# Float32 products on halves of the array in place of high and low parts

## The chip, the cores and the metric

The kernel runs on one core of one Trainium2 chip. The metric is device time in microseconds, as the median of several executions; a separate execution is recorded by the hardware profiler, and all rows below come from that one. PE is TensorE (matrix products), PEld its weight loads, DVE is VectorE, ACT is ScalarE, POOL is GpSimd, SP is the engine that issues the transfers. SBUF is the on-chip working memory and PSUM the eight banks of 128 partitions x 512 float32 into which TensorE writes.

## The reference

Random-feature attention, and behind it a feed-forward layer with softplus. The inputs are float32 except the two weights of the feed-forward, which the kernel gets as float64 words.

```python
# q, k, v: (8, 8, 576, 64); omega: (128, 64); w_in: (512, 2048); w_out: (2048, 512)
q_s, k_s = q * D ** -0.25, k * D ** -0.25
def phi(x):
    h = x @ omega.T - sum(x * x) / 2
    return exp(h - max(h)) / sqrt(128)
q_p, k_p = phi(q_s), phi(k_s)              # (b, h, 576, 128)
kv = k_p.T @ v;  z = sum(k_p)              # per head: 128 x 64, 128
x  = (q_p @ kv) / (q_p @ z + 1e-6)         # heads side by side: 4608 x 512
g  = softplus(x @ w_in)
out = g @ w_out                            # 4608 x 512
```

## The kernel before

**Feed-forward.** The 4608 tokens are taken in 13 blocks, three of 256 tokens and ten of 384. A block goes in 16 steps, one for each 128 of the 2048 hidden features. In a step the first layer multiplies four chunks of 128 inputs; each float32 operand is held as two float32r parts, a high and a low one, and three of the four products of parts are made (lines 765 to 767: 12 matmuls on the block's tokens). ScalarE and VectorE make the softplus of the result out of PSUM (771, 774, 777, 780), split it into parts (784, 788), and the second layer multiplies them with three matmuls of 512 columns for each 128 tokens (794 to 796), which add up in PSUM over the 16 steps.

**Attention.** Four heads make a quad, two quads a batch, so there are 16 quads. A quad's keys or queries are handled in five units, four of two 128-token tiles and one of one tile (of two heads side by side). A tile holds two heads: the transposed rows of one head on partitions 0 to 63, those of the other on 64 to 127. A unit is loaded, projected with omega, its row maxima and norms are taken, and ScalarE makes the exponentials (440), one instruction for each of the unit's columns of heads. Keys: the exponentials are multiplied with v and a column of ones (514), which adds up over a quad to kv and z. Queries: VectorE sums the products with z (595), inverts (600), POOL divides (604), TensorE transposes (611), and the result is multiplied with kv (673 and 674) to give the feed-forward's input, which is written as a high part `xh` (699) and a low part `xl` (702).

**Two forms of the projection.** For the first two batches (`NB = 2`; four quads) `project` (397) multiplies a tile by a 128 x 256 matrix in float32 that holds omega twice, with zeros between, so that both heads come out of one product. For the other six batches the transposed rows are loaded twice, on both halves of the partitions (331), rounded to a high part (364), and the low part takes the place of one half (368); `project_two` (407) then multiplies both parts at once with each part of omega, ScalarE copies one half of the result (414), and VectorE adds the other to it and takes the maximum on the way (419). The rows for the norms are loaded once more (355) and squared (375 or 377). Likewise only the first batch (`FN = 1`) multiplies queries with kv in float32 (`plan_x`, 723): two matmuls with 64 columns of weights, one for each half of the array's columns. The others split the queries (626, 630) and kv (538, 544), make four matmuls for each pair of heads (673, 674), and fold the halves with a copy (679) and an addition (682).

**Order.** All instructions of an engine stand in one order, written out before the kernel runs. Each piece of work (`Work`) has the engines that can do it with a cost for each, a due time, what it follows, and the buffers that it takes and gives back. `in_order` simulates the engines with these costs: the engine that can start first takes the earliest due of the works that can start, and a buffer is taken by the one that starts. Due times of attention spread it over about the first five sixths of the feed-forward's steps. PSUM's eight banks are named: two `at`, two `h` (first layer), three `acc` (second layer), one `kv`. Attention of the first batch may take any of `at`, `h` and `acc`; the later batches take `at` alone. SP issues the loads in the order of the plan, and a load waits for its buffer.

Of the kernel before, what the change touches and what calls it, by code (L numbers as in the profile page):

```python
# [28 lines left out]
FN = 1  # L29
NB = 2           # the batches before which the tensor engine has time to spare  # L30
RING = 2 * S     # tokens that the feed-forward's input holds
# [7 lines left out]
SLOW = 6.83      # until when the tensor engine's clock is at half its rate  # L39
# [4 lines left out]
CK, CQ = 0, 1  # L44
VW = (256 if CK else 512) + 4 * (D + 1)   # of one unit of the first batch: the heads' transposed keys, then their values
# [23 lines left out]
def in_order(works, room, ahead, margin):  # L69
    """The works in an order that keeps the engines busy: each engine, once free, takes the  # L70
    earliest due of those that can start. room: the buffers of each kind; ahead: how far from
    the earliest one left a work may be due; margin: how late data may come to the tensor engine."""
# [7 lines left out]
    held = {}          # buffer: the times from and to which it is taken  # L80
# [4 lines left out]
    def start(w):  # L85
        """when, where and with which buffers"""
# [41 lines left out]
def with_fill(out, held, banks, until, emit):  # L128
    """The same with something for the tensor engine to do where it waits, lest its clock go down"""
# [14 lines left out]
def favor_softplus_kernel(ctx, tc, q0, k0, qx, kx, qs, ks, qn, kn, vv, om, om2, wi, wo, out):  # L144
# [19 lines left out]
    idle = at.tile([P, P], F32, name="idle", tag="hl.0", bufs=1)  # L164
# [10 lines left out]
    # the features' weights, high and low parts: of one head on both halves of the rows; of two heads,  # L175
    # zeros between, for the first batches, where later the last rows of theirs go
    oms = const.tile([P, 2, M], F32R, name="oms")
# [11 lines left out]
    # each [P, DM] chunk of the weights: its float64 words, then in their place its two parts  # L189
# [27 lines left out]
    two = {}  # L217

    def load_two():
        two["f"] = ff.tile([P, 512], F32, name="omf2", tag=two["t"], bufs=1)[:, :M]  # L220
        nc.sync.dma_start(two["f"], om2)

    def two_parts():
        f = two["f"]
        nc.vector.tensor_scalar(f, f, float(D) ** -0.25, None, ALU.mult)
        nc.vector.tensor_copy(oms[:, 0], f)
        nc.vector.tensor_tensor(oms[:, 1], f, oms[:, 0].bitcast(F32), ALU.subtract)

    two_done = do("SP", 0.55, 81.62, load_two, take=[("t2", two, "t")], delay=DL)
    two_done = do("DVE", 0.5, 81.62, two_parts, after=[two_done], give=[(two, "t")])  # L230

    in_w = []          # the words that come where the parts go have gone

    def plan_weights(nm, fc, due):
        """float64 words to float32, rounded, in place; then to two float32r parts, exactly"""
# [4 lines left out]
        def load():  # L240
            # all chunks' parts fill the buffers: the last words are in another
# [5 lines left out]
        def low_bits(e):  # L247
            # the three bits of the low word that float32 has room for, rounded
# [6 lines left out]
        def rebias(e):  # L255
            # the exponent from a bias of 1023 to one of 127: what is under 2**-119 goes to zero
# [44 lines left out]
    # ---- attention: one quad = four heads = two pairs of heads  # L301
# [9 lines left out]
    prev = {}          # the latest unit's works: units follow each other  # L311

    def plan_unit(q, kind, u, due, early):
        """one unit of a quad's keys or queries: [P tokens, (head parity, pair), M]"""
        nm = f"{kind}{q.nm}_{u}"
        first = q.b < NB
        cols = early and {"k": CK, "q": CQ}[kind]
        if first:
            src = (k0 if kind == "k" else q0)[q.qd] if early else (kx if kind == "k" else qx)[q.b - 1, q.qd]
        else:  # L320
            src, src_nat = ((ks, kn) if kind == "k" else (qs, qn))
            src, src_nat = src[q.b - NB, q.qd], src_nat[q.b - NB, q.qd]
# [4 lines left out]
        def load():  # L327
            if not first:
                x = at.tile([P, UW], F32, name=f"x{nm}", tag=b["x"], bufs=1)[:, : n * P]
                for r in range(2):  # L330
                    nc.sync.dma_start(x[r * D : (r + 1) * D], src[:, u * UW : u * UW + n * P])
                b["raw"] = x
                return
            if early:
                # the exponentials come where the rows were
# [4 lines left out]
                if cols:  # L340
                    b["raw"], b["nat"] = x[:, 2 * P : 2 * P + w], x[:, :w]
                    c = VW if kind == "k" else w
                    nc.sync.dma_start(x[:, 2 * P : 2 * P + c], src[:, u * (VW if kind == "k" else 2 * P) :][:, :c])
                else:
                    c = VW if kind == "k" else UW
                    b["raw"], b["nat"] = x[:, :w], x[:, w : 2 * w].rearrange("p (c d) -> p c d", d=D)
                    nc.sync.dma_start(x[:, :c], src[:, u * c : u * c + c])
# [5 lines left out]
        def load_nat():  # L353
            b["nat"] = at.tile([P, 4, D], F32, name=f"n{nm}", tag=b["nats"], bufs=1)[:, :n]
            nc.sync.dma_start(b["nat"], src_nat[:, 4 * u : 4 * u + n])

# [3 lines left out]

        def high(e):
            t = at.tile([P, 4 * P], F32R, name=f"hl{nm}", tag=b["hls"], bufs=1)
            b["hi"], b["lo"] = t[:, : n * P], t[D:, : n * P]
            (nc.scalar.copy if e == "ACT" else nc.vector.tensor_copy)(b["hi"], b["raw"])
# [649 lines left out]
```

## Time and profile before

| | |
|---|---|
| three executions | 1172.12, 1176.93 (median), 1177.15 us |
| span of the profiled execution | 1173.2 us |
| PE, busy in the span | 1090.2 us (93%) |
| PEld | 969.7 us (83%) |
| DVE | 839.2 us (72%) |
| ACT | 778.8 us (66%) |
| POOL | 597.7 us (51%) |
| moved by DMA | 93.09 MB |

The page gives no time beside the span for the profiled execution; its span lies 3.7 us under the median of the three. Matmuls overlap, since each has a long way through the array: a matmul's duration is not what it costs, and the distance from its start to the start of the next one is. That is why 93% busy does not say how full PE is. In the timeline, a row of several instructions (x4) has the start of the first one and the time up to the end of the last.

### The profile page before, as it was taken

To read this page: it belongs to the slowest core of one execution; us is meant where nothing else is said; L and a number is where in the kernel's file an instruction comes from. 1 tells how busy PE (TensorE), PEld (TensorE's weight loads), DVE (VectorE), ACT (ScalarE), POOL (GpSimd) and SP (SyncE) were. 2 spreads that over 40 slices of the span, in tenths; PEclk is the share of its full clock that TensorE was granted. 3 is DMA by queue.
4 is the path that set the end of the run, shared out by engine and by line. 5 is a ranking of instruction groups with operands and counts; after the bars stand their busy time and mean duration, and the time that the engine had idled before them with its cause. 6 is when DMAs were issued, how large, how long until landed. Compare 5 with 4: busy or idle time off the path is not lost.

```text
span 1173.2 us, 20521 instructions
## 1 busy us (share of the span) xinstructions
PE 1090.2 (93%) x6094; PEld 969.7 (83%) x6094; DVE 839.2 (72%) x2842; ACT 778.8 (66%) x2061; POOL 597.7 (51%) x630
## 2 busy tenths in 40 slices
PE   8776889999998899999999999999998999999998
PEld 8655778888787788888898898888897888899997
DVE  7999997788878877877777777877786788311111
ACT  5566667777776666677777786666675667555544
POOL 4657764555555555555456555455553454322222
PEclk8889889999999999999999999999999999999999
DMA  9642123342323232232332231332222220000000
GB/s 356 226 127 90 42 77 89 80 113 79 86 79 94 68 100 57 71 100 64 78 88 75 64 105 57 82 92 60 73 85 69 58 82 23 1 28 1 28 1 28
DMA packets 66543, 93.09 MB, mean 79 GB/s; under 512 B 10880, under 2 KB 40320, under 8 KB 66432
## 3 DMA queue, kind: packets, MB, share of 16 engines
q1 hardware_dynamic: 66432, 91.78, 26.7%
q8 instruction: 49, 0.80, 0.3%
q14 instruction: 62, 0.51, 0.1%
HBM read 82.28 MB, written 9.47 MB: 78 GB/s over the span
## 4 chain that ended last, share of the span: by engine, by line
PE 44%; DVE 36%; ACT 11%; issue 6%; DMA 2%; POOL 1%; SPq 0%; DVEq 0%; ACTq 0%; POOLq 0%
DVE junk L595 7%; PE h L765 6%; PE h L766 6%; PE h L767 6%; PE acc L794 6%; PE acc L795 6%; PE acc L796 6%; ACT phk L440 3%; PE kv L514 3%; DVE smk L433 2%; DVE u L780 2%; DVE phq L419 2%; DVE phk L419 2%; ACT phq L440 2%; DVE smk L428 2%
## 5 line engine op out<-in xcount | busy, mean ns | idle before, releaser
L788 POOL TENSOR_TENSOR gl<-u,gh 128x384 fp32r<-128x384 f32 (+1 forms) x205 | 202.0, 986 | 280.0 <-ACT gh L784 219.5
L765 PE MATMUL h<-xh,wi 128*128 128x384 f32 (+1 forms) x832 | 278.8, 335 | 17.9 <-DVE u L780 17.7
L766 PE MATMUL h<-xl,wi 128*128 128x384 f32 (+1 forms) x832 | 272.2, 327 | 1.0 <-DVE xl L731 1.0
L767 PE MATMUL h<-xh,wi 128*128 128x384 f32 (+1 forms) x832 | 271.9, 327 | 0.0
L794 PE MATMUL acc<-wo,gh 128*128 128x512 f32 x576 | 230.9, 401 | 0.0
L795 PE MATMUL acc<-wo,gh 128*128 128x512 f32 x576 | 226.1, 392 | 1.2 <-DVE wo L280 1.2
L796 PE MATMUL acc<-wo,gl 128*128 128x512 f32 x576 | 225.7, 392 | 0.0
L780 DVE SCALAR_TENSOR_TENSOR u<-h,u 128x384 f32<-128x384 f32 (+1 forms) x208 | 108.5, 522 | 160.7 <-ACT u L777 157.4
L765 PEld LDWEIGHTS h<-xh,wi 128*128 128x128 f32 x832 | 159.2, 191 | 27.5 <-DVE u L780 22.8
L771 ACT ACTIVATE u<-h 128x384 f32<-128x384 f32 (+1 forms) x208 | 96.9, 466 | 124.3 <-PE h L767 104.4
L595 DVE CUSTOM_DVE_ANT_0 junk<-phq,zb 128x128 f32<-128x128 f32 x280 | 149.2, 533 | 29.8 <-ACT phq L440 4.2
L766 PEld LDWEIGHTS h<-xl,wi 128*128 128x128 f32 x832 | 159.5, 192 | 5.0 <-DVE xl L731 1.2
L767 PEld LDWEIGHTS h<-xh,wi 128*128 128x128 f32 x832 | 159.2, 191 | 0.0
L796 PEld LDWEIGHTS acc<-wo,gl 128*128 128x128 f32 x576 | 108.6, 188 | 24.3 <-POOL gl L788 0.3
L795 PEld LDWEIGHTS acc<-wo,gh 128*128 128x128 f32 x576 | 108.8, 189 | 14.7 <-DVE wo L280 1.7
L794 PEld LDWEIGHTS acc<-wo,gh 128*128 128x128 f32 x576 | 108.8, 189 | 13.9 <-issue 0.5
L440 ACT ACTIVATE phk<-phk,smk 128x128 f32<-128x128 f32 x216 | 69.8, 391 | 75.2 <-DVE smk L433 71.7
L604 POOL TENSOR_TENSOR phq<-phq,dnq 128x512 f32<-128x512 f32 (+1 forms) x69 | 66.3, 962 | 84.2 <-DVE dnq L600 49.7
L774 ACT ACTIVATE u<-u 128x384 f32<-128x384 f32 (+1 forms) x208 | 104.4, 502 | 4.3
L440 ACT ACTIVATE phq<-phq,smq 128x128 f32<-128x128 f32 x216 | 69.8, 392 | 55.6 <-DVE smq L433 55.4
L777 ACT ACTIVATE u<-u 128x384 f32<-128x384 f32 (+1 forms) x208 | 104.4, 502 | 3.5
L784 ACT CAST gh<-u 128x384 fp32r<-128x384 f32 (+1 forms) x181 | 87.8, 485 | 28.0 <-DVE u L780 17.4
(130 smaller groups left out, 2012.3 us busy)
## 6 DMA issues: line engine op xcount, KB each, us to landing
xk<-ks SPq DMA_DIRECT2D x96, 128.0 KB, 2.7
xq<-qs SPq DMA_DIRECT2D x96, 128.0 KB, 2.8
out<-o SPq DMA_DIRECT2D x36, 256.0 KB, 2.1
vk<-vv SPq DMA_DIRECT2D x70, 130.0 KB, 2.4
rawi<-wi SPq DMA_DIRECT2D x16, 512.0 KB, 6.2
rawo<-wo SPq DMA_DIRECT2D x16, 512.0 KB, 4.3
nk<-kn SPq DMA_DIRECT2D x48, 128.0 KB, 2.4
nq<-qn SPq DMA_DIRECT2D x48, 128.0 KB, 2.6
```

Source lines behind the costliest of these rows:

```text
L440: nc.scalar.activation(b["ph"][:, c], x[:, c], AF.Exp, bias=b["sm"][:, 2, c : c + 1])
L595: nc.vector.tensor_tensor_reduce((b["junk"][:, c] if "junk" in b else junk)[r], b["ph"][r, c], q.zb[r, h], 1.0, 1e-6, ALU.mult, ALU.add, d ...
L765: nc.tensor.matmul(b["h"], wh, xh[:, cc, t], start=cc == 0, stop=False)
L766: nc.tensor.matmul(b["h"], wh, xl[:, cc, t], start=False, stop=False)
L767: nc.tensor.matmul(b["h"], wl, xh[:, cc, t], start=False, stop=cc == NCC - 1)
L774: nc.scalar.activation(b["u"], b["u"], AF.Exp, scale=-1.0)
L777: nc.scalar.activation(b["u"], b["u"], AF.Ln, bias=1.0)
L780: nc.vector.scalar_tensor_tensor(b["u"], b["h"], 0.0, b["u"], ALU.max, ALU.add)
L788: (nc.vector if e == "DVE" else nc.gpsimd).tensor_tensor(b["gl"], b["u"], b["gh"].bitcast(F32), ALU.subtract)
L794: nc.tensor.matmul(acc[tt], gh, w2[fc][:, 0], start=fc == 0, stop=False)
L795: nc.tensor.matmul(acc[tt], gh, w2[fc][:, 1], start=False, stop=False)
L796: nc.tensor.matmul(acc[tt], gl, w2[fc][:, 0], start=False, stop=fc == NFC - 1)
```

## The change

The features' products are made in float32 for all eight batches, and so are the products of queries and kv; high and low parts stay in the feed-forward only.

- Projection: for each tile two matmuls in place of one or two. Each takes one head: 64 rows of the array (partitions 0 to 63, or 64 to 127), the head's transposed rows as weights, omega as the moving operand with 128 columns. The two write to two banks, one for each head, so a unit takes two banks at once, and gives them back when its exponentials are done. The maxima are taken by two reductions, one for each bank; the exponentials read PSUM.
- Queries times kv: `plan_x`, unchanged, for all batches. The splits of rows, queries and kv, the copies and additions that joined the parts, and the second and third load of the rows are gone. The low part `xl` is now always made by VectorE, out of PSUM.
- z goes through memory transposed, so that each head's z lies in consecutive words when VectorE reads it.
- Four buffers of rows (`x`) instead of two. The second batch may use the `acc` banks too (`more`).
- Costs in the plan: the diff has them.

```diff
     def act(n, space=None):
-        return (0.054 if space == PSUM else 0.094) + 0.000833 * n
+        return (0.066 if space == PSUM else 0.105) + 0.000833 * n
...
         def project():
+            both = [bank(f"pp{nm}_{j}", b["ppb", j]) for j in range(2)]
+            b["pp"] = [x[:, : nt * M].rearrange("p (t m) -> p t m", m=M) for x in both]
+            b["rest"] = both[0][:, 2 * M :]
             for t in range(nt):
-                o = b["pp"][:, 2 * t : 2 * t + 2, :]
-                nc.tensor.matmul(o, b["raw"][:, t * P : (t + 1) * P], omf, start=True, stop=True)
+                for j in range(2):
+                    r = slice(j * D, (j + 1) * D)
+                    nc.tensor.matmul(
+                        b["pp"][j][:, t], b["raw"][r, t * P : (t + 1) * P], omf[r, j * M : (j + 1) * M],
+                        start=True, stop=True,
+                    )
+            if cols:
+                b["sm"] = at.tile([P, 3, 4], F32, name=f"sm{nm}", tag=b["sms"], bufs=1)
+                b["ss"] = b["rest"][:, :n]
+                for t in range(nt):
+                    nc.tensor.matmul(
+                        b["ss"][:, 2 * t : 2 * t + 2], b["nat"][:, t * P : (t + 1) * P], halves, start=True, stop=True
+                    )
-        def maxima():
-            nc.vector.tensor_reduce(b["sm"][:, 1, :n], b["pp"][:, :n], AX.X, ALU.max)
-        def project_two(t):
...
-        def aside(t):
...
-        def sums(t):
...
+        def maxima(j):
+            nc.vector.tensor_reduce(b["sm"][:, 1, j:n:2], b["pp"][j], AX.X, ALU.max)
...
-            x = b["pp"] if first else b["ph"]
-            for c in range(n):
-                nc.scalar.activation(b["ph"][:, c], x[:, c], AF.Exp, bias=b["sm"][:, 2, c : c + 1])
+            for t in range(nt):
+                for j in range(2):
+                    c = 2 * t + j
+                    nc.scalar.activation(b["ph"][:, c], b["pp"][j][:, t], AF.Exp, bias=b["sm"][:, 2, c : c + 1])
...
+        kind_ = BANKS.get(q.b, "at")        # BANKS = {0: "any", 1: "more"}
+        p = do(
+            "PE", 0.12 + (0.44 if cols else 0.215) * nt, due + 0.53, project, after=[ld] + ([s] if cols else []),
+            behind=prev.get("project"),
+            take=[(kind_, b, ("ppb", 0)), (kind_, b, ("ppb", 1))] + (sm if cols else []) + ([] if early else [("ph", b, "phs")]),
+        )
...
+        m = do("DVE", dve(nt * M), due + 0.01, lambda: maxima(0), after=[p, r])
+        m = do("DVE", dve(nt * M), due + 0.01, lambda: maxima(1), after=[m], give=[] if early else [(b, "x")])
         m = do("DVE", dve(n), due + 0.41, less_norms, after=[m])
-        m = do("DVE", dve(n), due + 0.42, bias, after=[m], give=[(b, "ssb")] if cols else [])
+        m = do("DVE", dve(n), due + 0.42, bias, after=[m])
         e = do(
-            "ACT", n * (act(M, PSUM if first else None) + 0.09), due + 0.42, exponent, after=[m],
-            give=[(b, "sms")] + ([(b, "ppb")] if first else []),
+            "ACT", n * 0.26, due + 0.42, exponent, after=[m],
+            give=[(b, "sms"), (b, ("ppb", 0)), (b, ("ppb", 1))],
         )
...
         def out_z():
-            q.zd = dram.tile([P, 4], F32, name=f"zd{q.nm}", tag="zd", bufs=2)
-            nc.sync.dma_start(q.zd, q.z)
+            q.zd = dram.tile([4, M], F32, name=f"zd{q.nm}", tag="zd", bufs=2)
+            nc.sync.dma_start(q.zd.rearrange("c m -> m c"), q.z)
...
         for p in range(2):
-            cc = 2 * q.qd + p
-            if q.b < FN:
-                plan_x(q, due, cc, o, w, t0, any_, qt, p)
-                continue
...
+            plan_x(q, due, 2 * q.qd + p, o, w, t0, any_, qt, p)
...
-                "PE", 0.0025 * n + 0.013, due, lambda ccs=ccs: layer1(ccs),
+                "PE", 0.00254 * n + 0.063, due, lambda ccs=ccs: layer1(ccs),
-                "PE", 0.653, due + 6.38, lambda tt=tt: layer2(tt),
+                "PE", 0.68, due + 6.38, lambda tt=tt: layer2(tt),
...
-    counts = {"w": 2 * NFC, "t2": NT2, "x": 2, "nat": 2, "v": 2, "hl": 2, "sm": 4, "ph": 4, "z": 2, "zb": 2, "dn": 4}
+    counts = {"w": 2 * NFC, "t2": NT2, "x": 4, "v": 2, "sm": 4, "ph": 4, "z": 2, "zb": 2, "dn": 4}
...
+    room["more"] = room["at"] + room["acc"]
```

More of the change, by code (lines that the diff above doesn't have):

```diff
@@ L214, in do @@
         return w
[L217 to L230, printed above, removed]
     in_w = []
@@ L450, in plan_unit @@
             ldv = do("SP", 0.55, due - 5.26 + .1, load_v, behind=ld, take=[("v", b, "vs")], delay=DL)
-        lds = ld
-        if not first:
-            lds = do("SP", 0.55, due - 3.95, load_nat, behind=ld, take=[("nat", b, "nats")], delay=DL)
-        wx, h, l = n * P, None, None
-        s = do(("POOL", "ACT"), (pool(w), act(w)), due, squares, after=[lds])
-        if not first:
-            h = do(
-                ("DVE", "ACT"), (dve(wx, 2), act(wx)), due, high, after=[ld], behind=prev.get("high"),
-                take=[("hl", b, "hls")],
-            )
-            l = do(
-                ("DVE", "POOL"), (dve(wx), pool(wx)), due + 0.1, low, after=[h], behind=prev.get("low"), give=[(b, "x")],
-            )
-            prev.update({"high": h, "low": l})
@@ new lines, in plan_unit @@
+        s = do(("POOL", "ACT"), (pool(w), act(w)), due, squares, after=[ld])
+        r, sm = None, [("sm", b, "sms")]
+        if not cols:
+            r = do("DVE", dve(w), due + 0.2, norms, after=[s], behind=prev.get("norms"), take=sm)
+            prev["norms"] = r
+        kind_ = BANKS.get(q.b, "at")
[4 more added lines that the diff above has]
+        )
@@ L518, in plan_keys @@
         q.kvm = do(
-            "PE", 0.855, due + 1.6, outer, after=[e, ldv, q.kvm], take=[("acc" if q.n == 1 else "kv", q.slots, "kv")] if u == 0 else [],
+            "PE", 0.9, due + 1.6, outer, after=[e, ldv, q.kvm], take=[("acc" if q.n == 1 else "kv", q.slots, "kv")] if u == 0 else [],
             give=[(b, "x")] if early else [(b, "phs"), (b, "vs")],
@@ L645, in plan_queries @@
         h = do(
-            ("ACT", "DVE"), (act(n * M, PSUM), dve(n * M)), due + 1.1, high, after=[t],
-            give=[(b, "tpb")] if q.b < FN else [],
-        )
-        if q.b >= FN:
-            h = do("DVE", 0.6, due + 1.1 + .1, low, after=[h], give=[(b, "tpb")])
+            ("ACT", "DVE"), (act(n * M, PSUM), dve(n * M)), due + 1.1, turned, after=[t], give=[(b, "tpb")],
+        )
         q.turned.append(h)
```

226 lines of the change are left out of this document (34 added, 192 removed).

## The prediction

> **What bounds the kernel now.** I read the stages first, because the work changes twice. The windows give busy time for each engine in each stretch; the second line names the columns.
>
> ```profile
> core 0 of [0], span 1173.2 us
> core 0: us, PE busy (x) PEld busy (x) DVE busy (x) ACT busy (x) POOL busy (x), PEclk, DMA share, GB/s
> 0.00:200.00 200.00, 161.49 (x911) 138.39 (x912) 186.46 (x434) 123.54 (x342) 124.49 (x122) 0.90 0.43 144
> 200.00:1000.00 800.00, 760.05 (x4328) 677.96 (x4326) 622.02 (x2349) 567.64 (x1541) 428.62 (x464) 1.00 0.28 77
> 1000.00:1173.00 173.00, 168.62 (x858) 153.33 (x858) 30.73 (x62) 87.60 (x178) 44.56 (x45) 1.00 0.04 14
> ```
>
> DVE fills the first 200 us (186 of 200). The last 173 us hold the feed-forward almost alone. The 800 us between hold all attention of batches 2 to 7, and there no engine is full. The same windows for line 765 alone, four of whose matmuls make a step of the feed-forward, show how many steps each stretch did:
>
> ```profile
> 0.00:200.00 200.00, 32.58 (x99) 20.59 (x99) 0.90 0.43 144
> 200.00:1000.00 800.00, 194.21 (x580) 109.67 (x580) 1.00 0.28 77
> ```
>
> PE's timeline gives what a step costs, from start to start: one step of the tail, four products of 256 columns, and a stretch with one projection, four transposes and eight products of keys with v.
>
> ```profile
> 1080.64 0.34 PE L765 MATMUL h<-xh,wi 128*128 128x384 f32 x1
> ...
> 1082.73 0.39 PE L794 MATMUL acc<-wo,gh 128*128 128x512 f32 x1
> ...
> 1084.77 0.34 PE L765 MATMUL h<-xh,wi 128*128 128x384 f32 x1
> ```
>
> ```profile
> 598.11 0.28 PE L673 MATMUL xp<-qhq,kvs 128*128 128x256 f32 x1
> ...
> 598.58 0.34 PE L765 MATMUL h<-xh,wi 128*128 128x384 f32 x1
> ```
>
> ```profile
> 608.84 0.63 PE L407 MATMUL ppq<-oms,hlq 128*128 128x256 f32 x4
> 609.31 0.34 PE L765 MATMUL h<-xh,wi 128*128 128x384 f32 x1
> ...
> 611.05 0.60 PE L611 MATMUL tpq<-ident,phq 128*128 128x128 f32 x4
> 611.48 1.00 PE L514 MATMUL kv<-vk,phk 128*128 128x65 f32 x8
> 612.29 0.48 PE L794 MATMUL acc<-wo,gh 128*128 128x512 f32 x1
> ```
>
> A step of 384 tokens takes 4.13 us. One of 256 has 12 matmuls of 0.117 (0.47 / 4) and six of 0.227 (2.04 / 9): 2.77. The 580 matmuls are 145 steps. There are 48 small steps, 99 / 4 = 25 of them done before, so 23 x 2.77 + 122 x 4.13 = 568 us of the 800. Attention on PE, by the code's counts for a quad: 18 tiles of projection at 0.235, five times 0.9 for kv (0.81, and 0.09 by which the next matmul's row is longer than its like), 18 transposes at 0.11, eight products of 0.117 and eight of 320 columns, 0.147 in proportion: 4.2 + 4.5 + 2.0 + 2.1 = 12.8, for 12 quads 154. So PE computes 722 us and waits 78 in this stage. How the waits go with DVE is seen in two stretches; first all engines, then line 765:
>
> ```profile
> 400.00:500.00 100.00, 93.31 (x513) 82.39 (x514) 77.65 (x281) 66.64 (x178) 54.22 (x59) 1.00 0.30 78
> 600.00:700.00 100.00, 97.94 (x561) 89.43 (x560) 72.34 (x293) 76.55 (x205) 56.20 (x61) 1.00 0.32 90
> ```
>
> ```profile
> 400.00:500.00 100.00, 23.00 (x68) 12.95 (x69) 1.00 0.30 78
> 600.00:700.00 100.00, 24.88 (x73) 13.70 (x73) 1.00 0.32 90
> ```
>
> 17 steps are 70 us, with a share of 154 / 8 = 19 for attention 89: 11 us of waits at DVE 78%. 18.25 steps leave 5.5 at DVE 72%. The bound of the stage is PE's own work plus waits for a chain that runs through DVE, ACT and POOL.
>
> **What leaves those engines.** The groups of the whole kernel (busy, mean ns | idle before):
>
> ```profile
> L419 DVE CUSTOM_DVE_ANT_0 phk<-ppk,phk 128x128 f32<-128x128 f32 x216 | 52.0, 283 | 3.9 <-ACT phk L414 3.4
> L682 DVE TENSOR_TENSOR x<-xp,x 64x256 f32<-64x256 f32 (+1 forms) x112 | 50.9, 454 | 37.6 <-ACT x L679 35.7
> L630 DVE TENSOR_TENSOR qlq<-tpq,qhq 128x512 fp32r<-128x512 f32 (+1 forms) x84 | 45.1, 551 | 30.7 <-ACT qhq L626 30.5
> L364 DVE CAST hlk<-xk 128x512 fp32r<-128x512 f32 (+1 forms) x40 | 24.1, 603 | 5.6 <-PE ppk L407 5.2
> L368 POOL TENSOR_TENSOR hlk<-xk,hlk 64x512 fp32r<-64x512 f32 (+1 forms) x57 | 67.5, 1183 | 24.4 <-ACT hlk L364 5.4 <-issue 4.1 <-DVE hlk L364 3.9
> L702 POOL TENSOR_TENSOR xl<-x,xh 128x256 fp32r<-128x256 f32 (+1 forms) x56 | 46.0, 825 | 41.9 <-ACT xh L699 36.3 <-PE ppq L407 5.2 <-PE xp L674 0.2
> L731 DVE TENSOR_TENSOR xl<-xp,xh 128x256 fp32r<-128x256 f32 (+1 forms) x8 | 3.5, 445 | 0.0
> ```
>
> L419, L364 and L368 have a twin for queries of about the same size. DVE loses 2 x 52 + 51 + 45 + 2 x 24 = 248. It gains `xl`, 56 x 0.445 = 25, and 240 reductions, two for a unit. One of 256 columns out of PSUM is the smallest of line 400, 0.39 us; 240 x 0.39 = 94 at most, since a fifth are half as wide:
>
> ```profile
> L400 DVE TENSOR_REDUCE smk<-ppk x20: 387/678/683, 6.6 to 192.6; 128x4 f32<-128x512 f32 x16, 128x2 f32<-128x256 f32 x4
> ```
>
> Net -129, nearly all in the stage: 622 becomes 493, 62% of 800. ACT loses the copies of lines 414 and 679, POOL 2 x 67.5 + 46 = 181 of its 598 (the three stretches' sum). DVE gains once more from that: its tiny bias instruction takes 0.13 us where it starts at once and 0.45 in the median, and I ascribe the difference to POOL's use of the memory that both read; the bound from below is no gain.
>
> ```profile
> L428 DVE SCALAR_TENSOR_TENSOR smk<-smk x80: 132/450/1260, 7.6 to 955.8; 128x4 f32<-128x4 f32 x64, 128x2 f32<-128x2 f32 x16
> ```
>
> So DVE ends near 55 to 60%. Two stretches give 5.5 us of waits less for 5 points of DVE, which can't go on to below zero; what remains even in the good stretch are hand-overs. I take 3 in 100 us, half of the good stretch, thus 24 in the stage; the bounds are 0 and the 78 of now.
>
> The third load of the rows and the second copy leave SP's queue (one transfer for a unit in place of three, 240 fewer), and a load there is queued no longer behind POOL's splits. That I cost at nothing: DMA is 28% busy. The transposed z costs SP a transfer in pieces of four bytes, 14 times, under the units of the next quad's keys; should it land late, line 595 of one unit waits on DVE, 14 times, and PE with it only if the next transposes are due by then.
>
> **What PE gains and loses.** The trace has no matmul on half of the rows. It has the kin on half of the columns, line 723; PE, then PEld:
>
> ```profile
> 92.00 1.30 PE L723 MATMUL xp<-qq,kvs 128*64 128x320 f32 x8 [1.56 <-DVE xl L731]
> 93.23 0.50 PE L794 MATMUL acc<-wo,gh 128*128 128x512 f32 x1
> 93.57 0.39 PE L795 MATMUL acc<-wo,gh 128*128 128x512 f32 x1
> ```
>
> ```profile
> 93.23 0.19 PEld L794 LDWEIGHTS acc<-wo,gh 128*128 128x128 f32 x1 [0.49 <-issue]
> ```
>
> Four float32 products stand there as eight matmuls, two passes each. In fp32r a pass of 320 columns is 0.147 us, and eight one after the other at twice that (a float32 column at half the rate) would be 2.35. They took 1.23 to the next start: four pairs of 0.27, so the halves run at the same time. And there is a price: 1.23 - 4 x 0.267 leaves 0.16, of which some 0.05 is the first, half-wide weights' load and 0.1 an empty array; then the next matmul needs 0.34 to its successor in place of 0.227, because its weights were not loaded ahead. Leaving the halves costs 0.1 + 0.11 = 0.21 us. Entering full-width weights on half of the rows I take as the same 0.21, all entries here having stood in a wait; the bounds are 0 and 0.21.
>
> A two-tile unit then has four slots. A slot streams 128 float32 columns (0.267 x 128 / 320 = 0.107) under a load that takes as long (kv's slot, 0.9 / 8 = 0.11): 0.44 + 0.42 = 0.86 against 0.47 now. 96 such units x 0.39 and 24 of one tile x (0.22 + 0.42 - 0.235) = 0.4 are +47 us in the stage. Products with kv, two pairs of heads in one visit: 4 x 0.213 or 4 x 0.267 and 0.37 of entering and leaving, against 8 x 0.117 or 8 x 0.147: +0.28 or +0.26, 24 visits, +6 (and +9 more if every pair makes a visit of its own).
>
> The Trainium skill, TensorEngine Tiling (Array Packing), Key Properties, says that changing the tiling mode drains the TensorE, while other tiles of the same mode run independently; the exit at 93.23 agrees with its 0.1 us. By the page alone (drains without the reload) the stage would pay 120 x 0.2 = 24, an estimate, in place of 47, and end where half of the price does below.
>
> **The sum.** Stage: 568 + 154 + 47 + 6 + 24 = 799 against 800. First 200 us, bound by DVE: batch 1 loses L630, L682 and half a dozen small ones for five query units, 5 x (0.55 + 0.7), and gains 15 x 0.1 of reductions and 4 x 0.445 of `xl`: -3; z read in consecutive words saves 0.11 (369 to 255, the smallest of each kind) on 20 to 40 of line 595, -3. Its PE work in wide float32 projections (0.86 for a unit too) does not change. Tail: nothing, no part of it is touched.
>
> ```profile
> L595 DVE CUSTOM_DVE_ANT_0 junk<-phq,zb x280: 369/392/1509, 159.0 to 999.8; 128x128 f32<-128x128 f32 x112, 64x128 f32<-64x128 f32 x28
> L595 DVE CUSTOM_DVE_ANT_0 xq<-xq,zb x40: 255/281/1414, 30.6 to 78.4; 128x128 f32<-128x128 f32 x32, 64x128 f32<-64x128 f32 x8
> ```
>
> That is -7, and 1166 for the span of 1173.2. Not every change of mode is paid in full: where PE stands in a wait before a projection, the empty array lies in it, and I take off 3. Span 1163, and with the 3.7 us by which the median lies over this span, 1167.
>
> **Rivals.** (a) The switches cost little: row halves take weights ahead while full-width matmuls run. Then 47 + 6 falls to about 0, the stage is 568 + 154 + 24 = 746, the time 1173 - 54 - 9 + 4 = 1114; with half of the price 1140. For it: the trace shows the price on columns only. Against: the exit has the same neighbours. (b) Slower: banks. A unit takes both `at` banks from its projection to its last exponential: 0.86 + two reductions 0.8 + two tiny instructions 0.9 + four exponentials, about 1.2, and four hand-overs of 0.15 make 4.4 us, where a unit is due every 800 / 120 = 6.7, and transposes (0.6 and a copy) and kv products need the same two banks. It decides from about 2 us of queueing on DVE and ACT: then each projection, which stands in PE's fixed order, waits. At 0.3 us for each of 120: waits 24 + 36 = 60, span 1199, time 1203. For it: two banks replace one, held more than twice as long. Against: DVE and ACT get emptier. (c) Row halves don't run at the same time: 8 slots in place of four, +0.44 x 96 + 0.22 x 24 = +47, time 1214. Against: line 723. (d) The waits fall only to those of the good stretch, 5.5 in 100, 44 in all: 1167 + 20 = 1187, and with the half-price switches of (a) to 1160.
>
> **Chances.** Forecast 0.35, (a) 0.17, (b) 0.2, (c) 0.08, (d) 0.2. What a measurement of this kernel tells from no change is about 0.5%, 6 us. Of the forecast's 0.35 (1157 to 1177) 0.24 are faster, 0.11 within it; (a) is faster; (d) spreads over all three, 0.06, 0.07, 0.07; (b) and (c) slower. Together faster 0.47, same 0.18, slower 0.35. The range goes from half-way into (a) to (b): 1128 to 1203; the likeliest case's own is 1152 to 1180.
>
> **What would show it.** Right: projections start in pairs a few ns apart, a unit takes 0.44 us plus gaps, and the weights after it are loaded late, 0.2 us; DVE in the stage at 55 to 62%, POOL under 45%; PE's waits at 24 us, mainly before projections and transposes. Wrong: no gap after a projection (a); long waits of a projection on ACT's exponentials (b); starts 0.11 apart (c); DVE still over 70%, or the first 200 us changed by more than 15 us, which nothing here foresees.

## The result, and the profile after

The changed kernel takes 1275.97 us (median; 1274.27 to 1277.25) beside 1175.47 for the kernel before: a ratio of 1.0852, with a 95% interval of 1.0822 to 1.0881. It is slower by 100 us. The forecast was 1167, and 1275.97 lies outside its range. Of the kernels below, the first with an extra write was traced in an execution that took 1418 us at a granted clock of 0.735; its time leaves that execution out, its landing times come from it. The loss lies in the stage with attention. The windows of the kernel after (busy time per engine, then the granted clock, the DMA share and GB/s):

```profile
core 0: us, PE busy (x) PEld busy (x) DVE busy (x) ACT busy (x) POOL busy (x), PEclk, DMA share, GB/s
200.00:1000.00 800.00, 737.18 (x4348) 617.47 (x4347) 375.96 (x1339) 394.37 (x1040) 239.67 (x299) 0.95 0.27 54
200.00:1100.00 900.00, 828.14 (x4851) 693.13 (x4850) 423.74 (x1502) 444.06 (x1166) 269.20 (x334) 0.95 0.27 53
```

DVE, ACT and POOL did lose their work. But PE is idle for 72 of the 900 us, and its mean clock is 0.95 where it was 1.00. The same windows for line 595 of this kernel, one of the three products of the first layer, count the steps: 532 / 4 = 133 in 800 us, where the kernel before made 145.

```profile
200.00:1000.00 800.00, 183.84 (x532) 102.38 (x531) 0.95 0.27 54
```

The chain that ended last, from the page, has a share of transfers, and by line the first of them is the load of the queries' rows:

```profile
PE 73%; DMA 11%; DVE 9%; issue 4%; ACT 1%; POOL 1%; SPq 0%; POOLq 0%; DVEq 0%; ACTq 0%
PE acc L624 10%; PE h L595 10%; PE h L596 9%; PE h L597 9%; PE acc L625 9%; PE acc L626 9%; DMA xq<-qx 8%; PE kv L424 5%; PE ppq L348 4%; PE ppk L348 3%; PE xp L553 3%; PE tpq L506 2%; DVE xq L490 2%; DMA xk<-kx 1%; DMA zd<-z 1%
```

Among the DMA issues, z's write to memory stands out. The last number is the median time from issue to landing. The first fence is of before, the second of after, with the loads of the queries' rows for comparison:

```profile
zd<-z SPq DMA_DIRECT2D x14, 2.0 KB, 1.9
```

```profile
xq<-qx SPq DMA_DIRECT2D x56, 256.0 KB, 2.8
...
zd<-z SPq DMA_DIRECT2D x14, 2.0 KB, 10.3
```

The same 2 KB, 14 times, take 10.3 us instead of 1.9. The trace after tells the landing of one of the 14 only, but z's read, which waits for the write, is issued 9.9 to 12.6 us behind it all 14 times, and 1.4 to 4.4 us in the kernel before. What follows from one of them is seen around 626 us. SP's timeline after (start, duration, issue), then the chain in that stretch (start, us), then the timelines of PE, DVE and ACT:

```profile
626.46 0.38 SPq L460 DMA_DIRECT2D zd<-z  x1
626.93 0.46 SPq L325 DMA_DIRECT2D vk<-vv  x1
627.51 0.36 SPq L320 DMA_DIRECT2D xq<-qx  x1
638.03 0.33 SPq L464 DMA_DIRECT2D zb<-zd  x1
638.46 0.37 SPq L320 DMA_DIRECT2D xk<-kx  x1
```

```profile
627.51 12.81 DMA xq<-qx
...
640.39 0.62 POOL xq L332
641.01 2.13 issue
643.14 0.66 PE tpq L506 x2
```

```profile
635.77 0.34 PE L597 MATMUL h<-xh,wi 128*128 128x384 f32 x1
643.14 0.66 PE L506 MATMUL tpq<-ident,phq 128*128 128x128 f32 x2 [7.04 <-issue]
```

```profile
641.04 0.42 DVE L337 TENSOR_REDUCE smq<-xq 128x4 f32<-128x256 f32 x1 [8.52 <-POOL xq L332]
```

```profile
642.16 1.14 ACT L382 ACTIVATE phk<-ppk,smk 128x128 f32<-128x128 f32 x4 [9.37 <-DVE smk L374]
```

Two things happen at once. SP stands at `zb<-zd` (it needs z's write), with the load of the next keys behind it, until 638. And the queries' rows, issued at 627.51, before SP stood, are on their way for 12.81 us, where 2.8 is the median. POOL squares them late, and DVE, whose order is fixed, stands for 8.52 us at the sum of these squares (line 337). The unit of these rows is projected only at 651.83. But behind line 337, in DVE's order, stand the small norm instructions of the keys' unit before it, so ACT waits 9.37 us before the exponentials of that unit (line 382), and until they are done the unit holds both `at` banks. PE's next piece of work, two transposes, needs such a bank: its data were ready at 632, and it starts at 643.14, as the exponentials let go of the first bank. PE, whose order is fixed as well, stops for 7 us. That it waits for the bank is argued from the plan and these times; PE's row names no engine for the wait. DVE waits like this, for 7 to 8.5 us, behind each of the 13 writes of z after 200 us, once for a unit of keys and else for queries, whose waits add up to (us in all, times, longest):

```profile
DVE smq L337 <- POOL xq L332: 95.5, 13, 8.5
```

Behind the stop of PE the clock is lower for a while, as the windows around the same place show:

```profile
636.00:643.00 7.00, 0.10 (x1) 0.00 (x0) 1.30 (x5) 0.84 (x4) 1.11 (x2) 0.73 0.47 90
643.00:645.00 2.00, 1.86 (x10) 1.89 (x10) 0.42 (x1) 1.74 (x7) 1.07 (x2) 0.50 0.00 0
645.00:647.00 2.00, 2.00 (x7) 1.25 (x9) 0.56 (x1) 0.33 (x1) 0.00 (x0) 0.50 0.29 64
...
649.00:651.00 2.00, 2.00 (x10) 1.71 (x9) 0.55 (x2) 0.77 (x2) 0.00 (x0) 0.89 0.00 0
651.00:653.00 2.00, 2.00 (x17) 1.63 (x16) 0.43 (x2) 0.17 (x1) 1.00 (x1) 1.00 0.00 0
```

From 643 to 649 PE works at half its clock (the row left out has 0.50 too), and only from 651 at full. After 200 us PE's records have 14 gaps of over 1.3 us; they last 1.8 to 7.9 us, 71 us in all. All but the shortest begin 7 to 15 us behind one of these 13 writes, one for each. The Trainium skill, TensorE: Matmul & The Clock Gate, "HAM oscillation — how this bites in real kernels", warns of idle gaps beyond about 3.4 us, after which the clock falls to half; the 7 us gap and the 0.50 behind it agree. Shorter gaps have it here too: behind one of 2.90 us, from 1008.44, the clock is 0.50 from 1011.2 to 1018.0, while behind one of 2.61 us, from 429.18, it stays at 1.00.

### The profile page after: what moved, and what is told of

It reads as the page before. It is cut to its first block, busy times and chain, and to the rows that moved or that the text cites. A ratio compares the mean times of both kernels' runs of the same rounds, so it can differ in the third digit from the quotient of the medians.

```text
span 1273.4 us, 19784 instructions
## 1 busy us (share of the span) xinstructions
PE 1156.5 (91%) x6738; PEld 979.4 (77%) x6738; DVE 625.6 (49%) x1996; ACT 645.9 (51%) x1652; POOL 432.8 (34%) x492
## 4 chain that ended last, share of the span: by engine, by line
PE 73%; DMA 11%; DVE 9%; issue 4%; ACT 1%; POOL 1%; SPq 0%; POOLq 0%; DVEq 0%; ACTq 0%
PE acc L624 10%; PE h L595 10%; PE h L596 9%; PE h L597 9%; PE acc L625 9%; PE acc L626 9%; DMA xq<-qx 8%; PE kv L424 5%; PE ppq L348 4%; PE ppk L348 3%; PE xp L553 3%; PE tpq L506 2%; DVE xq L490 2%; DMA xk<-kx 1%; DMA zd<-z 1%
## 5 line engine op out<-in xcount | busy, mean ns | idle before, releaser
L618 POOL TENSOR_TENSOR gl<-u,gh 128x384 fp32r<-128x384 f32 (+1 forms) x206 | 198.2, 962 | 526.3 <-ACT gh L614 363.1
L595 PE MATMUL h<-xh,wi 128*128 128x384 f32 (+1 forms) x832 | 285.8, 343 | 17.6 <-DVE u L610 15.3
L597 PE MATMUL h<-xh,wi 128*128 128x384 f32 (+1 forms) x832 | 275.0, 331 | 0.3 <-POOL wi L260 0.3
L624 PE MATMUL acc<-wo,gh 128*128 128x512 f32 x576 | 246.4, 428 | 2.1 <-DVE xl L561 2.1
L626 PE MATMUL acc<-wo,gl 128*128 128x512 f32 x576 | 229.1, 398 | 0.3 <-POOL gl L618 0.3
L625 PE MATMUL acc<-wo,gh 128*128 128x512 f32 x576 | 229.2, 398 | 0.0
L595 PEld LDWEIGHTS h<-xh,wi 128*128 128x128 f32 x832 | 161.8, 195 | 39.4 <-DVE u L610 19.3
L597 PEld LDWEIGHTS h<-xh,wi 128*128 128x128 f32 x832 | 161.9, 195 | 0.5 <-POOL wi L260 0.5
L490 DVE CUSTOM_DVE_ANT_0 junk<-phq,zb 128x128 f32<-128x128 f32 x280 | 113.6, 406 | 56.3 <-ACT phq L382 31.6
L624 PEld LDWEIGHTS acc<-wo,gh 128*128 128x128 f32 x576 | 111.1, 193 | 38.3 <-issue 11.5
L625 PEld LDWEIGHTS acc<-wo,gh 128*128 128x128 f32 x576 | 111.3, 193 | 12.5
L614 ACT CAST gh<-u 128x384 fp32r<-128x384 f32 (+1 forms) x161 | 77.7, 483 | 80.6 <-PE acc L625 54.1
L382 ACT ACTIVATE phk<-ppk,smk 128x128 f32<-128x128 f32 x252 | 72.7, 370 | 85.0 <-DVE smk L374 80.7
L382 ACT ACTIVATE phq<-ppq,smq 128x128 f32<-128x128 f32 x252 | 72.6, 370 | 63.7 <-DVE smq L374 63.5
```

Source lines behind the costliest of these rows:

```text
L382: nc.scalar.activation(b["ph"][:, c], b["pp"][j][:, t], AF.Exp, bias=b["sm"][:, 2, c : c + 1])
L490: nc.vector.tensor_tensor_reduce((b["junk"][:, c] if "junk" in b else junk)[r], b["ph"][r, c], q.zb[r, h], 1.0, 1e-6, ALU.mult, ALU.add, d ...
L595: nc.tensor.matmul(b["h"], wh, xh[:, cc, t], start=cc == 0, stop=False)
L597: nc.tensor.matmul(b["h"], wl, xh[:, cc, t], start=False, stop=cc == NCC - 1)
L618: (nc.vector if e == "DVE" else nc.gpsimd).tensor_tensor(b["gl"], b["u"], b["gh"].bitcast(F32), ALU.subtract)
L624: nc.tensor.matmul(acc[tt], gh, w2[fc][:, 0], start=fc == 0, stop=False)
```

## The experiments

Each ratio is to the kernel before, with its 95% interval. The theory at the start: the transposed z's write is the whole loss, by landing late and holding up other loads. The rival: switching PE's rows, or holding two banks, costs more than forecast.

**The change with z as before.**

```diff
-            q.zd = dram.tile([4, M], F32, ...)
-            nc.sync.dma_start(q.zd.rearrange("c m -> m c"), q.z)
+            q.zd = dram.tile([P, 4], F32, ...)
+            nc.sync.dma_start(q.zd, q.z)
...
+            t = at.tile([P, M, 4], F32, ...)     # read as before, too
+            q.zb = t.rearrange("p m c -> p c m")
```

> The changed kernel with one part undone: z is written to memory as before, four floats for each feature side by side, and read back with a step of four; nothing else differs, and each engine's order stays. Theory A: the write of z in pieces of four bytes, 10 us to landing, holds up the loads behind it, PE then stands 3 to 8 us once for each of 14 quads (80 us in all gaps over 1.3 us of the middle stage) and runs at half clock after each. Then this kernel takes about 1170 us (1155 to 1190). Rival B: the loss is the switches between halves and full width, or the two banks; then it stays above 1240.

1165.5 us (1164.71 to 1168.37), ratio 0.9924 [0.9907, 0.9942]. Four lines of the change carry the whole loss and more: 110 us. The windows of this kernel, the steps of its first layer (line 593), z's write, and PE's longest wait from 200 to 1000 us:

```profile
0.00:200.00 200.00, 166.21 (x1074) 141.32 (x1075) 174.38 (x427) 119.15 (x322) 123.50 (x119) 0.87 0.41 143
200.00:1000.00 800.00, 796.72 (x4859) 669.77 (x4858) 447.83 (x1504) 446.43 (x1167) 274.95 (x333) 1.00 0.22 60
```

```profile
0.00:200.00 200.00, 30.49 (x96) 19.88 (x96) 0.87 0.41 143
200.00:1000.00 800.00, 201.89 (x592) 111.23 (x592) 1.00 0.22 60
```

```profile
zd<-z SPq DMA_DIRECT2D x14, 2.0 KB, 1.4
```

```profile
PE h L593 <- DVE u L608: 2.2, 1, 2.2
```

PE is idle for 3 of 800 us, at full clock. Against this kernel, the stretch from 200 to 1100 us after had 72 us without PE, where 800 to 900 us of this one have some 4. And the kernel after has 13 stretches at half clock there, 92 us by the trace's clock records; PE is busy in 70 of them, and half of that, 35, is lost. That is an estimate of 68 + 35 = 103, against 110 measured: about two thirds of it are PE's stops and one third the slow clock behind them, and 7 us are not accounted for.

**The kernel before, with the transposed z alone.** The same lines the other way round, in the kernel before.

> The kernel before with that one part done: z goes through memory transposed. Theory A: its loads are held up just so, 1230 to 1290 us. Rival B: z's way is worth nothing by itself or gains a little, since VectorE reads z faster: 1160 to 1180.

1236.74, ratio 1.0529 [1.0512, 1.0547]; z's write lands after a median of 9.6 us (eight of the 14 are told). The layout of z alone makes the old kernel 61 us slower, so the loss needs nothing of the projection. That it is less than 110 fits a PE that had 78 us of waits in this stage already, in which part of a stop can lie; how much of the difference is that, no run shows.

**The plan told of the late landing.** The writing order of the engines comes from costs; here the landing of z's write is 11 us in them, not 2.3.

```diff
-            r = do("SP", 0.55, due + 0.8, out_z, after=[a], give=[(q.slots, "z")], delay=DL)
+            r = do("SP", 0.55, due + 0.8, out_z, after=[a], give=[(q.slots, "z")], delay=11.0)
```

> The changed kernel, but the plan is told that the write of z lands after 11 us, so that it puts other loads on SP's queue ahead of z's way back. If only SP's queue is blocked (z's read waits for z's write, and loads stand behind the read), this cures most of it: 1165 to 1200 us. If the transfers themselves are held up behind the small pieces, loads that were issued right after the write still land late: 1210 to 1270.

1261.29, ratio 1.0741 [1.0712, 1.077]. SP's own queue no longer waits for z, but the load of the rows does, in POOL's waits (us in all, times, longest):

```profile
POOL xq L332 <- DMA xq<-qx: 132.5, 33, 7.2
```

After it was

```profile
POOL xq L332 <- DMA xq<-qx: 144.8, 35, 8.3
SPq L464 <- DMA zd<-z: 120.3, 13, 10.8
```

So taking SP's waiting at line 464 away is worth 15 us, and what remains points to the transfers themselves: while z's write is under way, the loads behind it land late.

**z without memory.** z goes to all partitions by a product with the identity on PE and a copy on ACT, as the first batch has it, for all batches.

```diff
-        if q.b:
+        if False:
...
-            "PE", 0.86, due + 0.8, rows, after=[a], take=[("any", q.slots, "zp"), ...
+            "PE", 0.86, due + 0.8, rows, after=[a], take=[(BANKS.get(q.b, "at"), q.slots, "zp"), ...
```

> The changed kernel with z brought to all partitions as the first batch has it: four float32 products with the identity on PE and a copy by ScalarE, no transfer at all; VectorE reads z in consecutive words. Theory A: as the one with z written straight, less what the faster sums are worth, plus 14 x 0.9 us of PE: 1160 to 1190 us. Rival B: above 1240.

1175.99, ratio 1.0 [0.9989, 1.001]: 100 us back, but 10.5 us above the version with z as before. DVE has z in consecutive words here as well, and its busy time in the stage falls from 447.83 to 415.31, yet no gain is seen from it: PE is full. The stage, and one of the 14 products in PE's timeline:

```profile
200.00:1000.00 800.00, 797.97 (x4889) 676.71 (x4888) 415.31 (x1468) 436.12 (x1141) 257.82 (x320) 1.00 0.19 55
```

```profile
584.72 1.05 PE L448 MATMUL zp<-ident,z 128*128 128x128 f32 x8
585.52 0.48 PE L624 MATMUL acc<-wo,gh 128*128 128x512 f32 x1
585.84 0.40 PE L625 MATMUL acc<-wo,gh 128*128 128x512 f32 x1
```

The product takes 0.80 to the next start, and that next matmul 0.32 where 0.227 is usual: 0.9 us, 14 times, 12.5 us, near the 10.5 measured.

**All 128 rows for a projection.** The version with z as before, but each product uses the whole tile as weights and omega beside zeros, instead of half of the rows.

```diff
-    b["pp"][j][:, t], b["raw"][r, t * P : (t + 1) * P], omf[r, j * M : (j + 1) * M],
+    b["pp"][j][:, t], b["raw"][:, t * P : (t + 1) * P], omf[:, j * M : (j + 1) * M],
```

> The kernel with z written straight, and the projections on all 128 rows: each head's matmul takes both heads' rows as weights and omega with zeros for the other head as the moving operand, so no change between halves and full width is needed, and nothing runs side by side. Order, banks and all else are the same. By the prediction's prices a two-tile unit then costs 8 x 0.11 = 0.88 us in place of 0.44 + 0.42, a one-tile unit 0.44 in place of 0.64: 96 x 0.02 - 24 x 0.2 = -3 us in the stage; 1160 to 1170 us in all. If the switches cost little and the halves are worth their time side by side, it loses 96 x 0.44 + 24 x 0.22 = 47: 1205 to 1220.

1167.13, ratio 0.9934 [0.9922, 0.9947], no different from halves of the rows (0.9924). PE's timeline of this kernel, and below it that of the kernel after, with halves:

```profile
516.73 0.34 PE L595 MATMUL h<-xh,wi 128*128 128x384 f32 x1
516.91 1.05 PE L348 MATMUL ppk<-omf,xk 128*128 128x128 f32 x8
517.72 0.42 PE L593 MATMUL h<-xh,wi 128*128 128x384 f32 x1
517.98 0.33 PE L594 MATMUL h<-xl,wi 128*128 128x384 f32 x1
```

```profile
800.22 0.34 PE L597 MATMUL h<-xh,wi 128*128 128x384 f32 x1
800.49 0.72 PE L348 MATMUL ppk<-omf,xk 64*128 64x128 f32 x8
801.13 0.44 PE L595 MATMUL h<-xh,wi 128*128 128x384 f32 x1
801.41 0.34 PE L596 MATMUL h<-xl,wi 128*128 128x384 f32 x1
```

A matmul of 384 columns has 0.173 us to its successor. With full rows the projection starts on time, takes 0.81 for its eight passes, and the next matmul 0.26 instead of 0.173: 0.90. With halves it starts 0.1 late (800.22 + 0.173 = 800.39), takes 0.64, and the next matmul 0.28: 0.1 + 0.64 + 0.11 = 0.85. What running two heads at once saves, the two switches take.

**Two units in one visit.** If the switches are the price, fewer visits save it. The projections of a unit of keys and one of queries go together, in the two banks that one unit had.

```diff
+            if mate:
+                mate["pp"] = [x[:, nt * M : 2 * nt * M].rearrange("p (t m) -> p t m", m=M) for x in both]
+            for c in ([mate] if mate else []) + [b]:
...
+        pair = not early and (4 <= m < len(quads) - 1 if kind == "q" else m >= 5)
```

> The kernel with z written straight, and the projections of a key unit and the query unit next to it made in one visit to the halves, in the same two banks (256 columns of each for the one, 256 for the other); 55 visits fewer of 126 in the middle stage. By the prediction's price of 0.42 us for a visit: 55 x 0.42 = 23 us less, 1140 to 1148, if PE stays as full as it is now (its waits 3 us in the stage). If the two banks, now held for both units, keep PE waiting: 1150 to 1175.

1146.16 (1145.29 to 1146.57), ratio 0.9751 [0.9738, 0.9763], the fastest version here. Its timeline:

```profile
515.75 0.39 PE L643 MATMUL acc<-wo,gl 128*128 128x512 f32 x1
516.07 0.72 PE L351 MATMUL ppq<-omf,xk 64*128 64x128 f32 x8
516.62 0.61 PE L351 MATMUL ppq<-omf,xq 64*128 64x128 f32 x8
517.16 0.44 PE L612 MATMUL h<-xh,wi 128*128 128x384 f32 x1
517.44 0.33 PE L613 MATMUL h<-xl,wi 128*128 128x384 f32 x1
```

The matmul ahead, with 512 columns, streams 0.227 us, so the visit reaches from 515.98 to 517.16, and the reload after it adds 0.11: 1.29 for two units, where two visits are 1.70. The kernel joins 55 pairs, and 19.3 us / 55 = 0.35 each were got of the 0.41.

**What is slow in the write.** Six kernels keep z as before (the 1165.5 version) and add one more write of the same 2 KB per quad, which nobody reads and on which nothing waits but the next use of two buffers, its own copy's in memory and z's, two quads on: such a kernel computes what the one before it does, and does one write more. They differ in the order of the pieces of four bytes and in their distance in memory.

```diff
             nc.sync.dma_start(q.zd, q.z)
+            zx = dram.tile([4, M], F32, ...)                                # side by side, transposed
+            nc.sync.dma_start(zx.rearrange("c m -> m c"), q.z)
...
+            zx = dram.tile([P, 4, 16], F32, ...)                            # 64 bytes apart, straight
+            nc.sync.dma_start(zx[:, :, 0], q.z)
...
+            zx = dram.tile([4, M, 16], F32, ...)                            # 64 bytes apart, transposed
+            nc.sync.dma_start(zx[:, :, 0].rearrange("c m -> m c"), q.z)
```

The last three have 2 or 8 in place of 16 as the last size: 8 and 32 bytes apart.

> The kernel with z written straight and read so; beside that write there is one more, of the same z, transposed in pieces of four bytes as in the changed kernel, which nobody reads. If the small pieces hold up the loads behind them, PE stands again once for a quad: 1210 to 1260 us. If what costs is that z itself comes late (its read, and the loads that stand behind that read in SP's queue, wait for it): 1163 to 1175.

> The same with the extra write laid out otherwise: 512 pieces of four bytes again, but 64 bytes apart, those of a partition next to each other. If the number of pieces costs: as with the transposed one, within 1%. If it is that neighbouring words come from different partitions: 1163 to 1175 us.

> The kernel with z written straight and an extra write of z that nobody reads, in the transposed order of the changed kernel (one head's 128 words, each from another partition, then the next head's), but with 64 bytes from word to word. If it is the order of the pieces that holds up the loads: 1210 to 1280 us, as with the extra transposed write. If it is that words of different partitions lie side by side: 1163 to 1175 us, as with the spread one.

> As the extra write 64 bytes apart, in the transposed order, but with 8 bytes from each piece to the next instead of 64: eight pieces, of eight partitions, now lie in each 64 bytes, and no two of them touch. What the extra write computes is read by nobody. Side by side, the extra write landed in 9.2 us and made 1268; 64 bytes apart in 3.3 us and 1167. If words that touch are the cause, it stays at 3 to 4 us and 1165 to 1172. If pieces of different partitions in one short stretch of memory are the cause, the landing rises with their number: half as many as side by side, so 5 to 7 us, and 1200 to 1240.

> The same with 32 bytes from each piece to the next: two pieces, of two partitions, in each 64 bytes. If words that touch are the cause: 3 to 4 us of landing and 1165 to 1172. If it is the number of pieces in a short stretch: little more than 64 bytes apart, 3.3 to 4.5 us, and 1165 to 1180.

> The extra write in the straight order, 8 bytes from each piece to the next: eight pieces in each 64 bytes as in the transposed one of 8 bytes, but they come from two partitions, four from each. If different partitions are what matters, 3 to 4.5 us of landing and 1165 to 1172. If the number of pieces in a short stretch counts wherever they come from, it is as slow as the transposed one of the same spacing.

| extra write | median us | ratio [95%] | landing, median us |
|---|---|---|---|
| transposed, side by side | 1265.62 | 1.0776 [1.0752, 1.08] | 9.2 |
| transposed, 8 bytes apart | 1169.68 | 0.9953 [0.9933, 0.9973] | 4.3 |
| transposed, 32 bytes apart | 1167.54 | 0.9931 [0.9909, 0.9954] | 3.3 |
| transposed, 64 bytes apart | 1167.43 | 0.9929 [0.9907, 0.9951] | 3.3 |
| straight, 64 bytes apart | 1168.6 | 0.9944 [0.993, 0.9958] | 3.6 |
| straight, 8 bytes apart | 1173.11 | 0.9983 [0.9971, 0.9995] | 3.9 |

The DMA issues that decide, of the first, the second and the fourth:

```profile
zx<-z SPq DMA_DIRECT2D x14, 2.0 KB, 9.2
```

```profile
zx<-z SPq DMA_DIRECT2D x14, 2.0 KB, 4.3
```

```profile
zx<-z SPq DMA_DIRECT2D x14, 2.0 KB, 3.3
```

The first of the six shows that nobody needs to wait for z: a write that is read by no one costs 100 us, more than the 45 to 95 that were expected of it. DVE stands at line 337 for the queries' rows in this kernel as well, 76.9 us in 14 waits. The other five have the same number of pieces, 512, and cost 2 to 8 us. So neither the number of small pieces nor the transposed order is the cause by itself; of the layouts tried, only the one in which pieces of four bytes from neighbouring partitions touch is slow. That it is the touching is not shown apart from the number of pieces in a stretch: side by side, 64 bytes hold 16 of them, 8 bytes apart eight. By that number, 8 bytes apart should have landed in 5 to 7 us and cost 35 to 75; it landed in 4.3 and cost 4. By touching words alone it should have landed in 3 to 4 and taken 1165 to 1172: the landing lies just above that, the time, 1169.68, within it. Most of the loss comes between 8 bytes apart and side by side. Straight pieces 8 bytes apart land faster than transposed ones, yet the kernel was 7.6 us slower with them, beside 4.2, and at 1173.11 just above what was expected; the intervals touch, and that isn't explained.

What in the path to memory makes this slow stays open. The packets of a slow write are recorded with 7 to 9 ns each, as those of a fast one are, and in the write at 480.88, the one whose landing of 10.3 us the trace after tells, the 512 have all started by 1.3 us behind its issue, so the records don't tell where the other 9 us go. The Trainium skill, DMA: Bandwidth & Descriptors, Specifications, says that transfers below 512 bytes are made by reading, modifying and writing; by that alone the pieces 64 bytes apart would be as slow, and they aren't.

## Why the prediction was wrong

**The step that failed** is a transfer that the sum costs at nothing: "The transposed z costs SP a transfer in pieces of four bytes, 14 times, under the units of the next quad's keys; should it land late, line 595 of one unit waits on DVE, 14 times, and PE with it only if the next transposes are due by then." The sentence ahead of it costs the loads of SP's queue at nothing as well, with "DMA is 28% busy". The transfer was seen, but its price was sought in the wrong place. The reductions with z (line 490 after) never wait for its read, and an unread write costs 100 us; SP's wait for z is worth 15. What hurts is that the loads issued behind the write land late, 12.81 us instead of 2.8. They stop DVE at line 337 for 7 to 8.5 us, and with it the units that stand behind in its order, until PE stops as well. The mean share of 28% says nothing of how long one transfer can delay others. The write was given no bound from above, and none of the rivals (a) to (d) has a transfer in it. Nor was the second cost in the sum: behind most stops of PE it works at half clock for 3 to 9 us (643 to 649 in the stretch above).

**The rest of the sum** can be judged on the version with z as before, 1165.5 against 1167.

- The price of a switch: 0.86 a two-tile unit was forecast; 0.85 is measured (800.39 to 801.13 and 0.11 behind). The pairs confirm its parts: the second unit of a visit adds 1.29 - 0.85 = 0.44, as forecast for four slots, which leaves 0.41 for entering and leaving, where 0.42 was forecast. Of this, the empty 0.1 ahead and the reload of 0.11 behind stand outside the eight passes, and 0.2 within their 0.64. Rival (a), cheap switches, is out, and so is (c): eight passes on halves take 0.64, where full rows take 0.81, and in the trace the two of a pair start 7 ns apart.
- Rival (b), banks: PE's waits from 200 to 1000 us don't name them; with 3 us of idle PE there is no room for 0.3 us on each of 120 projections. In the changed kernel itself they may well be the last link behind a late load, as said above.
- DVE 55 to 60% in the stage: 447.83 / 800 = 56%. POOL under 45%: 274.95 / 800 = 34%. PEclk stays 1.00.
- Waits of 24 us, from 0 to 78: 3 us. This term was too high by 21. Two stretches gave a slope, and hand-overs were assumed to remain at 3 in 100; with DVE at 56% PE is full. The stage did more in its 800 us than the sum has: 592 / 4 = 148 steps instead of 145, one of them more a small one (24 x 2.77 + 124 x 4.13 = 579 us instead of 568), and 126 visits of projections (PE's records) instead of 120, which with the attention that goes with them is 6 / 120 of 154 + 53, 10 us. Five of these six are no gain: the kernel before has them in the stage too, as 18 matmuls of line 397. The prediction's count left them out, so that 5 / 120 of 154, some 6 us, of the 78 it took for waits were work.
- The first 200 us: 6 us less were forecast, for DVE's sake. They did not come: 96 / 4 = 24 steps instead of 24.75, with DVE down from 186 to 174. So DVE was not all that bounds this stretch; that its mean clock is 0.87 where it was 0.90 may have a part in it, which no run tells apart. Less work was done here, 2 us of steps and 2 for a unit, so this stretch ends some 10 us behind the forecast. The stage did 13 us more work than before (11 of steps, 2 for a visit), where the forecast had it gain 4 (1 in the sum, 3 taken off): some 9 ahead of it. So 1165.5 beside 1167 holds two misses of some 10 us that cancel, and that it is so close is luck.
- z in consecutive words: 0.11 less for each reduction was forecast, from the smallest of each kind, and the group of line 490 after has a median of 293 ns where line 595 before had 392.

```profile
L490 DVE CUSTOM_DVE_ANT_0 junk<-phq,zb x280: 273/293/1109, 178.5 to 1114.8; 128x128 f32<-128x128 f32 x112, 64x128 f32<-64x128 f32 x28
```

The size was right, but DVE is not the bound once the splits are gone; the version with z over PE has that gain too and is slower by its products on PE.

## What to carry to other kernels

Never cost a changed transfer by its bytes or by the busy share of the DMA engines: look at how its pieces lie in memory, and if the trace has no such transfer, bound it from above by what stands in the same queue behind it, and by PE's clock after a stop. If a layout is changed only to spare an engine, ask first whether that engine is still the bound after the rest of the change. A price paid on entering and leaving a mode is paid for each visit, so joining visits paid here (0.35 us each), where other work inside a visit, full rows in place of halves, made no difference. And a late load delays more than its reader: here it held DVE at one instruction, and what stood behind that in its order stopped PE.

## What the runs showed of the hardware that was not expected

- 512 pieces of four bytes from 128 partitions, side by side in memory in transposed order, land after 9 to 10 us (medians); 32 or 64 bytes apart after 3.3; in straight order, in runs of 16 bytes, after 1.4 to 1.9. While they are under way, a load issued behind them took 12.81 us, and its issue was not held up.
- A stop of PE of 7 us is followed by some 6 us at half clock, so it costs about 10 us, an estimate. Stops of 2.67 to 3.09 us have half clock behind them as well; one of 2.61 has not.
- With float32 products of 128 columns, eight on halves of the rows in pairs take 0.85 us with their switches, and eight on full rows with zeros 0.90: the whole kernel can't tell them apart.
